# Cosformer attention and a mixture of adapters on one core: the written-out order of some 700 steps exchanged for another

## The chip, the cores and the metric

The kernel runs on 1 core of one Trainium2 chip. The metric is the device time of one execution in microseconds; what is given for a kernel is the median of several. The engines are called PE (TensorE: matmuls and transposes), DVE (VectorE), ACT (ScalarE), POOL (GpSimd) and SP (SyncE, which here issues every DMA). PEld is PE's loading of weights.

## The reference, cut to what matters

```python
B, H, S, D = 8, 8, 576, 64                     # q, k, v: [B, H, S, D], float32
theta = pi / 2 * arange(S) / S                 # c, s: its cosine and sine, one per position
phi = lambda x: concat([relu(x) * c, relu(x) * s], -1)
q_p, k_p = phi(q), phi(k)
kv  = einsum('bhsf,bhsd->bhfd', k_p, v)
z   = sum(k_p, axis=2)
attn = einsum('bhsf,bhfd->bhsd', q_p, kv) / (einsum('bhsf,bhf->bhs', q_p, z)[..., None] + 1e-6)

x = attn.transpose(0, 2, 1, 3).reshape(4608, 512)
logits = x @ w_gate                            # 8 experts
# the two largest logits of a row give the experts; w is their softmax
out = x + sum_over_the_two(w * (x @ A[e]) @ B[e])   # A[e]: 512 x 16, B[e]: 16 x 512
```

## The kernel before, in words

All eight heads of a batch lie side by side, and the 576 positions of a head are split as 64 partitions times 9 columns j, two heads' halves making 128 partitions. The batches come in load units: 0, 1, 2 and 3 alone, then 4 with 5 and 6 with 7 for q and k; v comes by single batches, but from batch 4 on its scaling treats two at once.

The work is cut into steps. `ops` holds each with its engines, its dependencies, the buffers that it takes and gives back, and a function that emits its instructions. The names, which the prediction uses:

| step | what it does | engine |
|---|---|---|
| `LKb`, `LQb`, `LVb`, `ldw` | loads of a unit of k, q, v; of the weights (L388, L356 to L361) | SP |
| `cKb.c`, `cQb.c` | a third of k or q cast to bf16, k with relu (L440, L442; L302 to L306) | DVE, ACT, for q also POOL |
| `phiKb.j`, `phiQb.j` | times tan: the sine half of a column (L310, L313) | POOL, DVE or ACT |
| `vsb.j` | a column of v times cos, as bf16 (L310, L313) | POOL, DVE or ACT |
| `kvb.c`, `keb` | 24 matmuls of batch b into two PSUM banks (L500); their copy to SBUF | PE; ACT or DVE |
| `tqi`, `eqi` | 8 transposes of phi(q) of tile i (L604); relu-copy of two tiles to SBUF (L621, L623) | PE; ACT or DVE |
| `ndi`, `rdi`, `nxi` | numerator and denominator of tile i (L647, L654, L662, L668); reciprocal; product, for two tiles (L692) | PE; DVE; DVE |
| `txi`, `exi` | 4 transposes of x (L713); copy of two tiles | PE; ACT or DVE |
| `zai` | x times A and w_gate (L738) | PE |
| `mxi`, `nt`, `ge`, `d`, `sg`, `w`, `zg` | largest logits (L749), their sum, mask, difference, sigmoid, weight, scaled z (L783), for three tiles; the last groups have two and one | DVE; `sg` ACT; `nt`, `w` DVE or POOL |
| `tz`, `ez` | transposes of the scaled z (L799); copy | PE; ACT or DVE |
| `dxi`, `eoi`, `sti` | x + z B in PSUM (L837); copy to the output buffer, two tiles wide or one; store (L855) | PE; ACT or DVE; SP |
| `fill=n` | n matmuls without use (L864) | PE |

There are 36 tiles of 128 rows: tiles 0 to 8 of batches 0 and 1, 9 to 17 of 2 and 3, 18 to 26 of 4 and 5, 27 to 35 of 6 and 7. Tiles 27 to 35 need `ke6` and `ke7`, that is the last loads V6 and V7 (`vs6.j` scales both at once).

The order is one text, `ORDER` (L68), read by `replay` (L127). In it `name=E@p` puts a step on engine E (V: DVE, S: ACT, G: POOL) and its result into place p of its buffers; a step without `=E` has one possible engine. Each engine gets its steps in the order of the text and runs them in that order; a step waits by semaphores for what it reads, and for the buffer that it overwrites. SP too works in order: a store whose tile is not ready holds all that stands behind it. Buffers that matter here: q has 4 places of a batch, k 4, v 3; PSUM has 8 banks; the output has 6 places, three of which lie in the first k tile and are free once batches 4 and 5 are cast. A place of the output is free again when its store has landed.

## Time and profile before

| | us |
|---|---|
| median of 3 runs | 119.18 (119.02 to 119.19) |
| the profiled execution | 118.97 |
| its span, first to last instruction | 117.2 |
| busy in the span: PE / PEld / DVE / ACT / POOL | 97.0 / 72.4 / 86.0 / 86.1 / 62.2 |
| granted TensorE clock, mean | 0.985 |

It moved 38.57 MB by DMA, 28.85 MB of it read from HBM. A store is 768 KB, but for two smaller ones at the end. To read the lines: a group of instructions gives line, engine, operation, what is written and read, shapes and count, then busy time in us and the mean ns of one, then the engine's idle time before them and what ended it. A line of the chain or of a timeline gives start, duration and what ran. "issue" is time in which an engine waited for nothing that the profile shows.

### The profile page before, as it was taken

Reading aid. Unit: us, or ns where it says so; the run is one execution under the profiler, and the core shown is the slowest. Engines: PE = TensorE matmul, PEld = TensorE weight load, DVE = VectorE, ACT = ScalarE, POOL = GpSimd, SP = SyncE. Lnnn points to the kernel's source line nnn. Section 1 sums busy time; section 2 is a strip of 40 time slices with the busy share of each in tenths; the row PEclk is TensorE's granted clock in tenths of the full one; section 3 lists DMA queues with packets and bytes.
Section 4 is the critical chain, followed back from the end, with each engine's and each line's share of the span. In section 5 each row is a group of like instructions: output and inputs, shape, how many; then the busy total and the mean of one; then the engine's idle time right before and its main releaser. Section 6 shows DMA issues by size and latency. Waiting matters only on the chain.

```text
span 117.2 us, 4510 instructions
## 1 busy us (share of the span) xinstructions
PE 97.0 (83%) x1930; PEld 72.4 (62%) x1939; DVE 86.0 (73%) x206; ACT 86.1 (73%) x132; POOL 62.2 (53%) x118
## 2 busy tenths in 40 slices
PE   5999687599885689698888969998879999999830
PEld 1344473479765586555767946787568797976300
DVE  1107878377958989799997886998499899987700
ACT  7328678479687797989838898777856666989750
POOL 3083707178889799379739954947993000011200
PEclk9999999976999999999999999999999999999999
DMA  2999999999999999999999999999810570493894
GB/s 42 401 399 391 390 392 392 392 304 395 392 389 391 391 391 391 385 393 389 388 393 385 392 385 391 388 417 424 363 56 6 233 299 19 168 369 163 336 394 187
DMA packets 15827, 38.57 MB, mean 329 GB/s; under 512 B 1728, under 2 KB 1728, under 8 KB 15808
## 3 DMA queue, kind: packets, MB, share of 16 engines
q1 hardware_dynamic: 15808, 38.29, 87.1%
q8 instruction: 15, 0.25, 0.9%
q14 instruction: 4, 0.03, 0.1%
HBM read 28.85 MB, written 9.44 MB: 327 GB/s over the span
## 4 chain that ended last, share of the span: by engine, by line
PE 32%; DMA 27%; DVE 21%; issue 6%; POOL 6%; ACT 2%; SPq 2%; DVEq 0%; POOLq 0%
DMA v<-in_v_dram 27%; PE psum L837 8%; PE psum L604 7%; PE psum L738 5%; DVE qt L623 5%; PE psum L713 4%; DVE x L692 4%; PE psum L654 3%; POOL vb L313 2%; POOL qp L304 2%; SPq L388 2%; DVE xt L306 2%; DVE kp L313 1%; DVE rd L687 1%; POOL qp L313 1%
## 5 line engine op out<-in xcount | busy, mean ns | idle before, releaser
L604 PE MATMUL psum<-ident,qp 128*128 128x128 bf16 x288 | 21.4, 226 | 4.1 <-DVE qp L313 1.3
L692 DVE TENSOR_TENSOR x<-psum,rd 128x1024 bf16<-128x1024 f32 (+1 forms) x19 | 22.2, 1168 | 0.6
L604 PEld LDWEIGHTS <-qp 128*128 128x128 bf16 x288 | 18.0, 101 | 6.1 <-issue 2.3
L313 POOL TENSOR_SCALAR kp<-kp,tanw 128x256 bf16<-128x256 bf16 (+1 forms) x28 | 16.2, 590 | 5.7 <-ACT kp L440 3.1
L313 POOL TENSOR_SCALAR qp<-qp,tanw 128x256 bf16<-128x256 bf16 (+1 forms) x31 | 17.2, 569 | 3.7 <-ACT qp L302 3.4
L313 POOL TENSOR_SCALAR vb<-v,cosw 128x256 bf16<-128x256 f32 (+1 forms) x25 | 14.8, 604 | 7.7 <-DMA v<-in_v_dram 7.6
L440 ACT ACTIVATE kp<-k 128x768 bf16<-128x768 f32 (+1 forms) x12 | 12.4, 1055 | 5.8 <-DMA k<-in_k_dram 5.4
L623 DVE TENSOR_SCALAR qt<-psum 128x2048 bf16<-128x2048 bf16 x12 | 14.6, 1214 | 0.9 <-PE psum L604 0.8
L713 PE MATMUL psum<-ident,x 128*128 128x128 bf16 x144 | 12.1, 221 | 3.3 <-DVE x L692 3.2
L500 PE MATMUL psum<-vb,kp 64*128 64x65 bf16 x576 | 12.8, 190 | 2.2 <-issue 1.1
L304 POOL CAST qp<-q 128x768 bf16<-128x768 f32 (+1 forms) x9 | 9.8, 1107 | 9.0 <-DMA q<-in_q_dram 7.4
L864 PE MATMUL psum<-ident 128*128 128x512 bf16 (+1 forms) x53 | 13.3, 405 | 1.4 <-POOL ident masks.py:199 1.4
L837 PE MATMUL psum<-x,ident 128*64 128x512 bf16 (+1 forms) x47 | 13.4, 384 | 0.6 <-ACT zt L302 0.3
L738 PE MATMUL psum<-AW,xt 128*128 128x136 bf16 x144 | 13.0, 223 | 0.7 <-DVE m L749 0.5
L500 PEld LDWEIGHTS <-kp 64*128 64x128 bf16 x576 | 10.2, 94 | 4.4 <-issue 2.4
L713 PEld LDWEIGHTS <-x 128*128 128x128 bf16 x144 | 9.3, 114 | 4.6 <-DVE x L692 4.3
L621 ACT ACTIVATE qt<-psum 128x2048 bf16<-128x2048 bf16 (+1 forms) x7 | 11.3, 1628 | 0.4 <-PE psum L604 0.4
L654 PE MATMUL psum<-kv,qt 128*64 128x65 bf16 x384 | 9.8, 197 | 2.1 <-issue 1.2
L837 PE MATMUL psum<-Bb,zt 128*64 128x512 bf16 (+1 forms) x42 | 11.4, 379 | 0.1
L302 ACT COPY o<-psum 128x1024 f32<-128x1024 f32 (+1 forms) x11 | 8.7, 821 | 3.7 <-PE psum L837 3.5
L738 PEld LDWEIGHTS <-xt 128*128 128x128 bf16 x144 | 9.4, 98 | 3.2 <-issue 1.4
L302 ACT CAST qp<-q 128x768 bf16<-128x768 f32 (+1 forms) x8 | 7.9, 987 | 4.7 <-DMA q<-in_q_dram 4.7
(60 smaller groups left out, 163.6 us busy)
## 6 DMA issues: line engine op xcount, KB each, us to landing
v<-in_v_dram SPq DMA_DIRECT2D x8, 1152.0 KB, 16.0
q<-in_q_dram SPq DMA_DIRECT2D x4, 1152.0 KB, 15.0
k<-in_k_dram SPq DMA_DIRECT2D x4, 1152.0 KB, 10.1
k<-in_k_dram SPq DMA_DIRECT2D x2, 2304.0 KB, 20.0
q<-in_q_dram SPq DMA_DIRECT2D x2, 2304.0 KB, 19.9
out_dram<-k SPq DMA_DIRECT2D x6, 768.0 KB, 4.5
out_dram<-o SPq DMA_DIRECT2D x5, 768.0 KB, 4.9
out_dram<-o SPq DMA_DIRECT2D x1, 512.0 KB, 2.7
```

What stands on the lines that cost most here:

```text
L302: nc.scalar.copy(o_ap, i_ap)
L313: eng.tensor_scalar(out=o_ap, in0=i_ap, scalar1=by, scalar2=0.0, op0=ALU.mult, op1=ALU.add)
L440: nc.scalar.activation(o_ap, i_ap, AF.Relu)
L500: nc.tensor.matmul(out=psum[:, s + hp, h2 * W:(h2 + 1) * W], lhsT=kp[hp * 64:hp * 64 + 64, bi * H2 + h2, :], rhs=vb_t[hp * 64:hp * 64 + 64 ...
L604: nc.tensor.transpose(out=o_ap[:, h2, :, hi, :], in_=qv[:, bi * H2 + h2, :], identity=ident)
L623: nc.vector.tensor_scalar(out=o_ap, in0=i_ap, scalar1=0.0, scalar2=None, op0=ALU.max)
L654: nc.tensor.matmul(out=psum[hi * 64:hi * 64 + 64, s + g, x * W:(x + 1) * W], lhsT=qt[:, qi, h2, hp, hi, :], rhs=kv_t[KV[b]["kv"].slot][:, ...
L692: nc.vector.tensor_tensor(out=x_t[Y["x"].slot][:, 0:n].rearrange("p n (g i d) -> p (n g) i d", g=2, i=4), in0=f()[:, :, :, 0:D], in1=r().t ...
L713: nc.tensor.transpose(out=bank16(s, 1024)[:, i * 512 + c * 128:i * 512 + (c + 1) * 128], in_=xv[:, c, :], identity=ident)
L738: nc.tensor.matmul(out=psum[:, s, i * ZW:(i + 1) * ZW], lhsT=xt_t[Z["xt"].slot][:, zi, c, :], rhs=AW[:, c, :], start=(c == 0 and i == 0), ...
L837: nc.tensor.matmul(out=o, lhsT=w, rhs=r, start=not last, stop=bool(last), skip_group_check=True)
L864: nc.tensor.matmul(out=psum[:, s % 8, c:], lhsT=ident, rhs=warm[:, c:], start=s < 8, stop=True, skip_group_check=True)
```

## The change

The text of `ORDER` is replaced; no other line differs. All steps of before are in it once, and the groups, tiles and matmuls are the same. What differs:

- the order of the steps on each engine, and the places in buffers and PSUM;
- the engine of some: `phiQ` of single batches runs 11 times on POOL, 9 on ACT, 16 on DVE (before 19, 10, 7), `phiK` 18, 11, 7 (15, 13, 8), `vs` 18, 12, 6 (16, 11, 9); of double units `phiQ` 9, 4, 5 (12, 5, 1), `phiK` 11, 4, 3 (13, 1, 4), `vs` 12, 4, 2 (9, 6, 3). `ex` runs 9 times on ACT and 10 on DVE (7 and 12), `ez` 4 and 9 (8 and 5), `eo` 21 and 3 (20 and 4), `eq` 7 and 12 as before, but other ones; `awb` is on POOL (ACT);
- five `fill` with 70 matmuls in all, instead of four with 55;
- the stores: before, `st8 st11 st14 st5` stand between the last load, `LV7`, and `kv6.0`, and then `st17 st20 st23 st2 st26 st29 st32 st35 st34`; now `st8 st14 st11 st17 st5 st2` stand there, and then `st23 st20 st26 st29 st32 st34 st35`.

The diff, cut to the first lines, those of `LQ4` and `LQ6`, and all from `LV7` on:

```diff
@@ ORDER @@
-half@3 ident fill=41@0 LQ0@3 LK0@0 LV0@0 pos tab LK1@1 LV1@1 LQ1@2 sig tan LQ2@1 ldw@2
-cQ0.0=S@0 cQ0.1=G@1 cQ0.2=G@2 LK2@2 phiQ0.5=G phiQ0.7=G LV2@2 cK0.2=S@1 cK0.1=V@2 cK0.0=V@3
...
-tx6@4 vs2.6=G d5 tx7 phiK2.7=S kv2.0@2 phiK2.3=G LV5@2 ex6=V@0 cK3.1=S@4 phiK2.8=G kv2.1 LQ4@2
...
-nd11 phiQ3.2=S kv3.0@0 fill=2@7 rd10@0 vs3.3=G LQ6@0 nx10@3 vs3.7=S vs3.5=G phiQ3.8=S nt8=G
...
-vs4.3=S kv4.0@0 vs4.7=G ez8=S@0 eq16=V@0 kv4.1 ex12=S@0 nt11=G kv4.2 LV7@1 d11 nd14@2 ke4=V@0
-sg11 nd15 w11=V dx6@0 rd14@1 nx14@6 dx7 dx8@6 eo6=S@4 cQ4.2=G@4 eo8=V nd16@2 tx14@0 zg11 st8.0
-tx15 za12@1 cQ4.0=G@2 ex14=S@1 nd17 mx12@2 kv5.0@6 rd16@2 nx16@7 za13 cQ4.1=S@0 za14 phiQ4.0=G
-kv5.1 mx13 mx14 kv5.2 phiQ4.1=S nt14=V phiQ4.4=G ge14 tq18@4 d14 ke5=V@2 sg14 phiQ4.7=G tq19
-phiQ4.2=S w14=V tx16@0 phiQ4.5=G tx17 zg14 eq18=S@1 ex16=V@0 tz14@6 phiQ4.3=G tz11@1 tq20@2
-ez11=V@1 za15@0 phiQ4.8=G cK6.0=V@2 tq21 ez14=S@2 cK6.2=S@0 nd18@4 dx11@1 eq20=V@0 phiK6.2=G
-nd19 cK6.1=S@4 phiK6.1=G mx15@1 dx9@2 rd18@0 dx10 nx18@0 za16 phiK6.5=G eo9=S@2 za17 mx16
-phiQ4.6=G tq22@4 mx17 nt17=V eo11=S tq23 d17 dx12@6 cQ6.0=G@0 sg17 st11.0 eq22=V@1 phiK6.3=S
-dx13 dx14@1 eo12=S@3 ge17 nd20@2 phiK6.6=G w17=V nd21 zg17 eo14=S tq24@6 phiK6.4=G rd20@2
-nx20@1 phiQ6.0=S tq25 st14.0 phiK6.0=G tx18@0 tx19 eq24=S@0 st5.0 phiK6.8=G ex18=V@0 nd22@2
-nd23 phiK6.7=V tq26@0 rd22@1 nx22@4 vs6.0=S@0,1 vs6.1=G za18@6 tx20@7 tx21 vs6.6=S tq27 vs6.2=G
-vs6.4=V tx22@2 tz17@3 vs6.3=S vs6.5=G tx23 ex20=V@1 za19 kv6.0@4 ez17=S@0 vs6.8=G ex22=V@0
-kv6.1 cQ6.2=S@2 za21@7 vs6.7=G eq26=V@1 dx15@2 cQ6.1=G@4 dx16 za20 mx18@1 eo15=S@5 za22 mx21@2
-za23 mx19 mx20 kv6.2 ge20 mx22 nt20=G phiQ6.2=V phiQ6.5=G nd24@0 ke6=S@1 d20 mx23 nd25 nt23=V
-sg20 kv7.0@4 d23 rd24@0 sg23 w20=G phiQ6.4=S nx24@2 phiQ6.7=G kv7.1 phiQ6.1=G kv7.2 ge23 w23=V
-phiQ6.8=G tq28@0 zg20 ke7=S@3 tq29 zg23 phiQ6.6=G tz20@6 nd26@2 eq28=V@0 ez20=S@1 nd27
-phiQ6.3=S dx17@7 rd26@0 dx18@0 nx26@5 eo17=S dx19 dx20@7 st17.0 eo18=S@4 tz23@6 nd28@2 eo20=V
-nd29 ez23=S@1 st20.0 tx24@0 rd28@0 tq30@6 nx28@3 tq31 tx25 tx26@1 ex24=S@0 eq30=V@0 tq32@2 tx27
-tq33 ex26=S@1 nd30@4 eq32=V@1 nd31 dx21@0 rd30@0 dx22 nx30@6 za24@2 eo21=S@2 za25 tx28@3 tx29
-za26 mx24@1 nd32@4 mx25 ex28=S@0 mx26 nt26=V nd33 ge26 d26 dx23@0 rd32@2 sg26 nx32@7 tq35@1
-w26=G eo23=S tq34@3 eq35=S@0 tx30@0 st23.0 tx31 zg26 za27@4 tx32@5 st2.0 ex30=V@1 za28 eq34=S@1
-za29 tz26@6 mx27@0 nd35@0 mx28 mx29 ez26=S@0 tx33 ge29 nt29=G rd35@0 za30@7 d29 dx24@2 nx35@0
-sg29 ex32=S@0 w29=G dx25 zg29 nd34@0 mx30@2 za31 eo24=S@5 rd34@0 za32 nx34@1 tz29@4 dx26@6
-ez29=S@1 mx31 za33@5 mx32 tx34@2 nt32=V eo26=S tx35@4 d32 dx27@0 mx33@1 ge32 sg32 st26.0
-ex34=V@1 dx28 ex35=S@0 w32=G za34 zg32 eo27=S@1 dx29@4 mx34 tz32@3 za35@6 nt34=G ez32=V@0
-eo29=S mx35@0 dx30@0 d34 nt35=G ge34 sg34 dx31 st29.0 d35 ge35 w34=G sg35 dx32@2 zg34 eo30=S@3
-w35=G zg35 eo32=V tz35@7 tz34@4 ez35=S@0 ez34=V@2 st32.0 dx35@7 dx33@0 eo35=S@0 dx34 st35.0
-eo33=S@2 st34.0
+half@3 ident fill=50@0 LQ0@3 LK0@0 LV0@0 pos tab LK1@1 LV1@1 LQ1@1 sig tan LQ2@0 ldw@2
+cQ0.0=V@0 cQ0.1=G@5 vone LK2@2 cQ0.2=G@3 phiQ0.1=G LV2@2 cK0.2=S@2 cK0.0=V@0 phiQ0.3=V
...
+phiK2.3=V tx4@2 tx6@3 phiK2.2=G eq8=V@1 sg2 LV5@2 tx5 tx7 phiK2.5=G cK3.2=S@1 kv2.0@4 LQ4@0
...
+vs3.2=G ez5=V@0 za8 cQ3.2=G@3 eq12=V@0 dx3@0 dx4 vs3.1=S vs3.4=G LQ6@2 dx5@6 mx6@0 eo3=S@2
...
+mx12@1 vs4.8=V nt11=G tx15 kv4.1 phiK4.8=V vs4.6=G ex14=V@1 eo8=S kv4.2 LV7@1 d11 mx13
+cQ4.0=S@4 cQ4.1=G@0 nd16@2 ge11 ke4=V@2 st8.0 nd17 za14 rd16@0 kv5.0@0 nx16@2 sg11 phiQ4.0=S
+w11=G phiQ4.2=G cQ4.2=S@2 kv5.1 phiQ4.4=V kv5.2 phiQ4.1=V mx14 tx16@2 phiQ4.5=V nt14=G tq18@4
+zg11 ke5=S@0 phiQ4.8=G tx17 tq19 ge14 d14 ex16=S@0 phiQ4.3=V za15@6 eq18=V@0 sg14 za16 w14=G
+za17 cK6.1=S@2 tz11@3 mx15@0 tq20@4 mx16 mx17 ez11=V@2 tq21 ge17 nd18@0 cK6.2=V@0 eq20=S@1
+phiK6.3=G zg14 nd19 phiK6.8=G nt17=V d17 tz14@7 rd18@2 sg17 tq22@4 phiK6.5=G ez14=S@0 nx18@1
+tq23 cK6.0=S@4 phiQ4.6=G dx11@7 w17=V dx9@2 eq22=V@0 dx10 phiK6.0=G tx18@0 eo9=S@3 tx19
+phiK6.4=V dx12@4 phiK6.7=G ex18=V@0 dx13 eo11=S cQ6.0=G@4 zg17 nd20@0 eo12=S@4 nd21 tz17@6
+rd20@0 za18@7 nx20@0 ez17=S@1 tq24@4 phiQ6.2=G phiK6.2=S dx14@6 cQ6.1=G@0 phiQ4.7=S nd22@0
+eo14=V nd23 mx18@0 tx20@6 st14.0 rd22@0 phiQ6.0=G tx21 phiQ6.3=S nx22@4 za19 st11.0 tq25
+phiQ6.1=G ex20=S@1 mx19 dx15@2 vs6.0=S@0,1 vs6.8=V vs6.4=G dx16 tq26@0 eq24=V@1 eo15=S@5 tq27
+vs6.5=G dx17@6 eq26=V@0 vs6.7=G nd24@2 eo17=S nd25 vs6.6=G phiK6.1=S za20 st17.0 rd24@0 tx22@6
+mx20 tq28@0 vs6.2=G vs6.1=S nx24@3 st5.0 tq29 nt20=G vs6.3=S tx23 st2.0 cQ6.2=G@2 d20 kv6.0@2
+ge20 sg20 ex22=V@0 phiQ6.4=S kv7.0@4 w20=V za21@6 phiK6.6=G eq28=S@1 zg20 za22 za23 mx21@1
+kv7.1 mx22 mx23 ge23 kv7.2 nt23=G d23 kv6.1 ke7=V@3 sg23 kv6.2 w23=G tz20@7 phiQ6.6=G zg23
+ke6=S@1 tq30@0 tz23@6 phiQ6.5=G ez20=S@2 nd26@2 ez23=V@0 nd27 phiQ6.8=V phiQ6.7=G dx18@6 rd26@0
+nx26@6 dx19 tq31 eo18=S@5 eq30=V@0 nd28@2 nd29 dx21@6 rd28@2 nx28@5 tx24@0 dx22 tx25 eo21=S@2
+tx26@1 tx27 ex24=V@0 nd30@2 nd31 dx20@0 rd30@1 nx30@2 tq32@6 eo20=S tq33 ex26=S@1 dx23@0
+eq32=V@1 za24@3 tx28@2 za25 eo23=S tx29 za26 mx24@2 ex28=S@0 nd32@4 st23.0 mx25 mx26 ge26 nd33
+nt26=V st20.0 d26 tq34@1 rd32@2 sg26 nx32@7 za27@0 w26=G eq34=S@0 tx30@2 za28 tx31 za29 mx27@1
+tx32@5 ex30=S@0 mx28 tx33 mx29 zg26 nd34@6 nt29=G ge29 ex32=S@1 tz26@4 rd34@0 tq35@1 d29 nx34@0
+za30@3 za31 sg29 ez26=V@0 za32 eq35=S@0 w29=G tx34@5 mx30@2 dx24@6 zg29 dx25 ex34=S@0 mx31 mx32
+tz29@4 nt32=V nd35@0 ge32 eo24=S@2 d32 ez29=V@1 dx26@5 rd35@0 za33@2 nx35@1 sg32 dx27@6 eo26=S
+w32=G dx28 zg32 st26.0 za34 eo27=S@1 mx33@0 tz32@4 mx34 dx29@3 ez32=V@2 nt34=G tx35@5 d34
+dx30@0 eo29=V ex35=S@0 dx31 ge34 sg34 st29.0 za35@4 eo30=S@4 w34=G dx32@6 mx35@1 zg34 nt35=V
+tz34@7 eo32=S ge35 ez34=V@2 d35 dx33@2 st32.0 sg35 dx34 w35=G zg35 eo33=S@2 tz35@0 ez35=V@0
+dx35@6 st34.0 eo35=S@0 st35.0
```

## Prediction

> **What bounds the kernel now.** I read the page first (its DMA digits: 40 slices of 2.93 us, 9 is full), then busy time by window, the chain of waits, and the SyncE timeline.

> ```profile
> DMA  2999999999999999999999999999810570493894
> ```
> ```profile
> 60.60:79.65 19.05, 16.87 (x404) 14.21 (x405) 15.91 (x35) 15.59 (x18) 13.78 (x17) 1.00 1.05 394
> 79.65:113.40 33.75, 30.22 (x631) 22.86 (x634) 26.59 (x71) 25.45 (x40) 10.68 (x21) 1.00 0.57 229
> ```
> ```profile
> 63.08 16.57 DMA v<-in_v_dram
> ...
> 112.33 1.01 ACT o L302
> ```
> ```profile
> 57.15 8.67 SPq L388 DMA_DIRECT2D v<-in_v_dram  x2
> 65.94 2.90 SPq L855 DMA_DIRECT2D out_dram<-k  x1
> ```

> The digits are 9 from the second slice to the 28th, up to 82 us: more than two thirds of the span run at the pace of the DMA engines. In the chain, the last load, V7, is issued at 63.08 and lands at 63.08 + 16.57 = 79.65. After it 33.7 us of computing remain, up to the last copy out of PSUM, 112.33 + 1.01 = 113.34; a store and the closing make it 117.2. The profiled execution took 118.97 us, 1.8 over its span and 0.2 under the median of 119.18. The windows list PE, PEld, DVE, ACT, POOL, the granted clock (1.00), DMA share and GB/s: in the tail PE is busy for 30.2 us of 33.75, DVE 26.6, ACT 25.5, POOL 10.7. No engine is full; they hand each tile round, every engine in a fixed order, and DVE has the longest list beside PE. So the time is V7's landing, plus this tail, plus the last store.

> **The loads do not move.** Both orders issue the same twenty loads (and the weights) in the same sequence, and all thirteen stores stand behind LV7 on SyncE. "Six stores instead of four" therefore means six stores ahead of kv6, none ahead of V7's bytes. V7 was issued 16.6 us before it landed: a load that a new buffer holds back must use up that lead first. LQ4 now waits for the casts of Q1 and Q2, and LV7 still for the scalings of V4 and V5, which in my walk end at about 59.5, as early as SyncE reaches LV7 in the row above. V7 lands at 79.7 in both.

> **Ahead of V7: does the work still fit?** The first cast of Q4 gives the start of the last stretch:

> ```profile
> 60.65 2.87 POOL L304 CAST qp<-q 128x1536 bf16<-128x1536 f32 x2 [2.69 <-DMA q<-in_q_dram]
> ```

> From here I summed each engine's steps up to its first step on V6, by the means of each kind. ACT has 15.5 us (13.6 before), POOL 12.2 (13.7), DVE the same as before within 0.1, and the window row shows that as 15.9 of 19.05. All fit. The 15 more filler matmuls lie ahead of V3's landing, where PE waits for loads; at 0.2 to 0.25 us each they would be 3 to 4 us on PE without that cover. The new order does more ahead of V6: za18, za19, tx20, tx21, ex20, tz17, ez17, cQ6.1 and three phiQ6; it leaves eq24, tq26, phiK6.1 and phiK6.6 for later.

> **The tail, walked by hand.** Durations, from the tail's groups by shape on DVE, ACT and POOL, the group of eq on ACT, and the chain for PE (x8 is one tq, two za, two tx; x2 one dx):

> ```profile
> L692 DVE TENSOR_TENSOR x<-psum,rd 128x1024 bf16<-128x1024 f32 x5 | 6.1, 1225 | 0.2
> L623 DVE TENSOR_SCALAR qt<-psum 128x2048 bf16<-128x2048 bf16 x4 | 4.9, 1218 | 0.2 <-PE psum L604 0.2
> L783 DVE TENSOR_TENSOR zg<-psum,w 128x384 bf16<-128x384 f32 x5 | 2.7, 549 | 0.1
> L749 DVE MAX8 m<-psum 128x8 f32<-128x8 f32 x18 | 2.4, 165 | 2.0 <-PE psum L738 1.8
> L306 DVE COPY xt<-psum 128x1024 bf16<-128x1024 bf16 x3 | 2.0, 684 | 0.2 <-PE psum L738 0.2
> ```
> ```profile
> L302 ACT COPY k<-psum 128x1024 f32<-128x1024 f32 x4 | 4.0, 1012 | 0.7 <-PE psum L837 0.6
> ...
> L302 ACT COPY o<-psum 128x512 f32<-128x512 f32 x3 | 1.8, 588 | 0.9 <-PE psum L837 0.7 <-PE psum L668 0.2
> ```
> ```profile
> L621 ACT ACTIVATE qt<-psum 128x2048 bf16<-128x2048 bf16 x5 | 9.3, 1867 | 0.4 <-PE psum L604 0.4
> ```
> ```profile
> L313 POOL TENSOR_SCALAR vb<-v,cosw 128x512 bf16<-128x512 f32 x5 | 3.7, 753 | 2.2 <-DMA v<-in_v_dram 2.2
> L313 POOL TENSOR_SCALAR qp<-qp,tanw 128x512 bf16<-128x512 bf16 x5 | 3.5, 720 | 0.0
> L304 POOL CAST qp<-q 128x1536 bf16<-128x1536 f32 x1 | 1.5, 1459 | 0.0
> ```
> ```profile
> 96.93 0.59 PE psum L837 x2
> 97.53 0.47 PE psum L738 x8
> 98.00 0.45 PE psum L713 x8
> ```

> Smaller steps, of 0.2 to 0.35 us, go in at their own means. For comparison the DVE timeline of before; the rows are nx24, nx26, nx32, then zg34 with zg35, and eo32:

> ```profile
> 86.44 1.23 DVE L692 TENSOR_TENSOR x<-psum,rd 128x1024 bf16<-128x1024 f32 x1
> ...
> 90.73 1.23 DVE L692 TENSOR_TENSOR x<-psum,rd 128x1024 bf16<-128x1024 f32 x1
> ...
> 99.75 1.22 DVE L692 TENSOR_TENSOR x<-psum,rd 128x1024 bf16<-128x1024 f32 x1
> ...
> 109.45 0.73 DVE L783 TENSOR_TENSOR zg<-psum,w 128x256 bf16<-128x256 f32 x2
> 110.10 0.68 DVE L306 COPY k<-psum 128x512 f32<-128x512 f32 x1
> ```

> After, from V7 on (times are ends):
> - DVE: vs6.8 80.5, eq24 81.6, eq26 82.7. PE waits for eq24, then nd24 and nd25 to 82.4; rd24 82.9, nx24 84.2. Before, nd24 stood behind kv6, and nx24 ended at 87.67: 3.5 us ahead here.
> - POOL: five scalings of V to 83.4, nt20 83.6, cQ6.2 85.0, phiK6.6 85.7. DVE: ex22 85.05. PE in a row: kv6.0, kv7.0, za21 to za23, kv7.1, kv7.2 (which needs phiK6.6), kv6.1, kv6.2, to 87.7. Tile 27 needs ke6 (88.4), and nd26 the banks of kv6 and kv7: here most of the 3.5 us is given back.
> - eq28 runs on ACT from 85.1 to 87.0 beside this; before, it was DVE's, directly ahead of nx26. nd26 and nd27 89.5, nx26 91.2 (before 91.96), eq30 92.3, nx28 93.8.
> - ex24 is DVE's now (0.68); nx30 96.4, eq32 97.5. Before, eq32 came ahead of nx30; now nd32 and nd33 wait for eq32, and nx32 ends at 100.4 (before 100.97): 0.6 ahead.
> - nx34 102.6; ACT: eo24 104.9, eo26 105.6; nx35 105.7, ex35 107.6, mx35 108.1, zg34 108.5, zg35 110.0 (before 109.45 + 0.73 = 110.18): 0.2 ahead.
> - The end. Before, eo32 (0.68) sat on DVE between zg35 and ez34, and dx33, dx34 and a wide eo33 came behind it: 110.18 to 113.34, 3.15 us. Now zg34, ez34, dx33 and dx34 lie in the wait for tile 35's sigmoid and product, eo32 is ACT's, and zg35 is followed by tz35 and ez35 (0.5, an estimate: an eighth of ex's columns), dx35 (0.35) and a narrow eo35 (0.59): 1.45 us, so 111.45. That gains 1.7 us.

> The last store leaves 0.2 + 1.7 = 1.9 us earlier.

> **What the walk leaves out** is PE standing at "issue", waiting for nothing that the profile shows:

> ```profile
> PEld L500 <- issue: 2.4, 5, 0.9
> PEld L604 <- issue: 2.3, 4, 1.0
> PEld L654 <- issue: 2.1, 3, 1.3
> ```

> (total us, times, longest.) L500 are the kv: 2.4 us over eight batches is 0.3 each. kv6 and kv7, with nothing behind them to hide a delay up to nx26, cost 0.6, and I add 0.1 for the rest of the way. Bounds: 0, if PE is waiting then anyway, and 2.4, all of L500's row. I take 0.7. [...]

> Forecast: 118.97 - 1.9 + 0.7 = **117.8 us**, its own range 117.0 to 118.6.

> **The rivals.**

> *A new wait for a store eats the gain.* eo33 now writes the buffer that eo26 filled last, so it waits until st26 has landed. Landing times of the stores in the tail, min, median, max:

> ```profile
> DMA to landing us min/median/max: 2.7/3.3/5.6
> ```

> eo26 ends at 105.6. With 3.3 the buffer is free at 109.0, and eo33, due at 109.85, doesn't notice. With 5.6 eo33 starts at 111.3 and the end is 1 us later; with a little more of "issue" that is 119.0, no change.

> *DVE reaches V7 late: slower.* The new order gives DVE 47 steps from SBUF to SBUF instead of 39, and beside POOL such a step takes longer:

> ```profile
> L313 DVE TENSOR_SCALAR kp<-kp,tanw 128x512 bf16<-128x512 bf16 x4 | 2.2, 570 | 0.0
> ...
> L313 DVE TENSOR_SCALAR qp<-qp,tanw 128x512 bf16<-128x512 bf16 x1 | 0.3, 343 | 0.0
> ```

> The same shape takes 343 ns in one place and 570 where POOL works on kp at the time. Nine such steps stand on DVE between V5 and V7; at 0.23 more each they are 2.1 us. With one PE stall of 1.3 ahead of an nx, and 1.0 of small waits, that is 4.4, against the 2.3 us that the walk leaves DVE before V7 (mx19 ends at 77.35): 2.1 late. Then eq24, nd24, za20 and mx20 are late; POOL, in order, holds nt20 and behind it cQ6.2 and phiK6.6; kv7.2, ke7 and tile 27 follow one for one: 119.9. It turns the gain into a loss from 1.4 us on, that is when nt20 ends after 85. For it: nothing in that chain can pass. Against it: the sums fit with 3 us to spare.
> [...]

> *The change isn't what it says*: did two stores pass ahead of V7, it would land later by two of 786 KB at the 394 GB/s of the window row, 4.0 us: 121.8. SyncE's order nearly excludes it.

> **How the numbers follow.** Forecast 0.62, new wait 0.13, DVE late 0.23, stores ahead 0.02. A measurement of this kernel tells about 0.2% (0.24 us) from no change. Faster is the forecast and half of the new wait (0.68); same is the other half and the edge of the third (0.08); slower the rest (0.24). The range runs from 116.6, the walk with no stall and 0.5 less of small waits than I put in, to 119.9, the time of DVE late.

> **What would show it.** V7 landing at 79.7; nx24 ending near 84.2, nt20 by 83.6; ke6 and ke7 done by 88.4; nx26 near 91; at the end one narrow copy of tile 35 that ends 1.5 us after the last zg. Should eo33 start over 0.3 us after dx34's end, the new wait is there. The prediction would be wrong with V7 landing late, with DVE still at its list ahead of V6 at 81, or with a PE stall over 1 us between 83 and 90, which moves all behind it.

## The result and the profile after

The changed kernel takes **118.00 us** (median of 4, 117.91 to 118.11); the kernel before, on the same chip, 119.12 (119.02 to 119.19). The ratio is 0.9907 (0.989 to 0.9924): 1.1 us faster, where 117.8 was forecast. The profiled execution took 118.06 us, 0.91 less than that of before, and its span is 116.3 (117.2). Each ratio here compares the fast executions alone; of the kernels below only the one with 24 idle matmuls fewer had slow ones, three of twelve.

Of after, the DMA digits of the page, two windows, and the chain of waits:

```profile
DMA  2999999999999999999999999999996001923994
```
```profile
60.60:79.65 19.05, 16.70 (x422) 13.52 (x414) 16.16 (x39) 16.65 (x21) 12.64 (x18) 1.00 1.05 396
79.65:112.50 32.85, 30.27 (x643) 22.84 (x640) 26.14 (x71) 24.23 (x36) 9.91 (x20) 1.00 0.59 236
```
```profile
63.30 16.49 DMA v<-in_v_dram
...
111.42 0.40 PE psum L837
111.83 0.02 issue
111.85 0.59 ACT o L302
```

V7 lands at 63.30 + 16.49 = 79.79, 0.14 behind before's. The DMA digits stay at 9 up to the thirtieth slice (28 before), since six stores now follow V7's bytes and not four. The tail ends at 111.85 + 0.59 = 112.44 with the copy of tile 35, 0.90 ahead of before's last copy. PE has the same work in the tail (30.27 against 30.22 us); the tail is shorter, and PE stands idle less.

The DVE timeline of after, the rows of nx24, nx26, nx28, nx32, then mx35, zg34, zg35 and the last ez:

```profile
82.84 1.22 DVE L692 TENSOR_TENSOR x<-psum,rd 128x1024 bf16<-128x1024 f32 x1
...
89.63 1.23 DVE L692 TENSOR_TENSOR x<-psum,rd 128x1024 bf16<-128x1024 f32 x1
...
92.84 1.23 DVE L692 TENSOR_TENSOR x<-psum,rd 128x1024 bf16<-128x1024 f32 x1
...
99.19 1.23 DVE L692 TENSOR_TENSOR x<-psum,rd 128x1024 bf16<-128x1024 f32 x1
...
108.60 0.17 DVE L749 MAX8 m<-psum 128x8 f32<-128x8 f32 x1 [0.56 <-PE psum L738]
108.69 0.41 DVE L783 TENSOR_TENSOR zg<-psum,w 128x256 bf16<-128x256 f32 x1
...
110.53 0.29 DVE L783 TENSOR_TENSOR zg<-psum,w 128x128 bf16<-128x128 f32 x1 [0.62 <-POOL w L780]
111.14 0.23 DVE L306 COPY zt<-psum 128x128 bf16<-128x128 bf16 x1 [0.32 <-PE psum L799]
```

Against before: nx24 starts 3.6 us earlier, nx26 1.1, nx32 0.56. zg35 is done at 110.82, 0.64 later than before's zg34 with zg35, and what stands behind it takes 1.62 us where before it took 3.16.

Between nx26 and nx28 PE's weight loads stand still inside nd28:

```profile
90.43 0.11 PEld L654 LDWEIGHTS <-qt 128*64 128x64 bf16 x1
90.91 0.20 PEld L654 LDWEIGHTS <-qt 128*64 128x64 bf16 x8 [0.37 <-issue]
91.84 0.20 PEld L654 LDWEIGHTS <-qt 128*64 128x64 bf16 x7 [0.73 <-issue]
```

The brackets give the idle time ahead of the row and what ended it. "issue": for 0.73 us PE waits for nothing that the profile shows, in the middle of sixteen loads that are all alike. (The 0.37 ahead of it is another matter: it stays where the 0.73 goes.)

### The profile page after: what moved, and what is told of

It reads as the page before. It is cut to its first block, busy times and chain, and to the rows that moved or that the text cites. A ratio compares the mean times of both kernels' runs of the same rounds, so it can differ in the third digit from the quotient of the medians.

```text
span 116.3 us, 4552 instructions
## 1 busy us (share of the span) xinstructions
PE 98.2 (84%) x1954; PEld 73.5 (63%) x1954; DVE 86.1 (74%) x211; ACT 84.1 (72%) x126; POOL 62.6 (54%) x119
## 4 chain that ended last, share of the span: by engine, by line
PE 36%; DMA 29%; DVE 14%; ACT 8%; SPq 4%; issue 4%; POOL 1%; POOLq 0%; DVEq 0%; ACTq 0%
DMA q<-in_q_dram 14%; DMA v<-in_v_dram 14%; PE psum L604 8%; DVE x L692 6%; PE psum L837 6%; PE psum L738 5%; PE psum L713 5%; SPq L388 4%; PE psum L654 4%; PE psum L500 4%; DVE qt L623 3%; ACT o L302 2%; PE psum L647 2%; ACT qt L621 2%; PE psum L799 1%
## 5 line engine op out<-in xcount | busy, mean ns | idle before, releaser
L604 PE MATMUL psum<-ident,qp 128*128 128x128 bf16 x288 | 21.5, 226 | 1.9 <-DVE qp L313 1.8
L692 DVE TENSOR_TENSOR x<-psum,rd 128x1024 bf16<-128x1024 f32 (+1 forms) x19 | 22.2, 1168 | 1.1 <-PE psum L864 0.6
L313 POOL TENSOR_SCALAR kp<-kp,tanw 128x256 bf16<-128x256 bf16 (+1 forms) x29 | 16.7, 587 | 10.0 <-ACT kp L440 10.0
L604 PEld LDWEIGHTS <-qp 128*128 128x128 bf16 x288 | 18.2, 102 | 3.1 <-DVE qp L313 1.9
L313 POOL TENSOR_SCALAR vb<-v,cosw 128x256 bf16<-128x256 f32 (+1 forms) x30 | 17.6, 604 | 3.1 <-DMA v<-in_v_dram 3.1
L864 PE MATMUL psum<-ident 128*128 128x512 bf16 (+1 forms) x70 | 16.4, 388 | 1.4 <-POOL ident masks.py:199 1.4
L623 DVE TENSOR_SCALAR qt<-psum 128x2048 bf16<-128x2048 bf16 x12 | 14.5, 1219 | 1.3 <-PE psum L604 1.2
L713 PE MATMUL psum<-ident,x 128*128 128x128 bf16 x144 | 12.5, 221 | 3.0 <-DVE x L692 2.8
L304 POOL CAST qp<-q 128x768 bf16<-128x768 f32 (+1 forms) x10 | 11.2, 1128 | 6.3 <-DMA q<-in_q_dram 6.3
L302 ACT COPY o<-psum 128x1024 f32<-128x1024 f32 (+1 forms) x12 | 9.9, 840 | 6.4 <-PE psum L837 6.2
L837 PE MATMUL psum<-x,ident 128*64 128x512 bf16 (+1 forms) x48 | 13.9, 385 | 0.6 <-DVE x L692 0.6
L837 PE MATMUL psum<-Bb,zt 128*64 128x512 bf16 (+1 forms) x48 | 13.8, 379 | 0.3 <-DVE zt L306 0.2
L713 PEld LDWEIGHTS <-x 128*128 128x128 bf16 x144 | 9.8, 114 | 6.1 <-DVE x L692 2.5
L738 PE MATMUL psum<-AW,xt 128*128 128x136 bf16 x144 | 12.7, 223 | 0.9 <-ACT xt L302 0.4
L621 ACT ACTIVATE qt<-psum 128x2048 bf16<-128x2048 bf16 (+1 forms) x7 | 11.4, 1628 | 2.2 <-PE psum L604 2.1
L313 POOL TENSOR_SCALAR qp<-qp,tanw 128x256 bf16<-128x256 bf16 (+1 forms) x20 | 11.5, 583 | 2.7 <-DVE qp L306 2.5
L500 PE MATMUL psum<-vb,kp 64*128 64x65 bf16 x576 | 11.7, 190 | 1.4 <-issue 0.6
L864 PEld LDWEIGHTS <-ident 128*128 128x128 bf16 x70 | 7.0, 104 | 9.1 <-issue 2.4
L780 POOL TENSOR_TENSOR w<-ge,ex 128x24 f32<-128x24 f32 (+2 forms) x10 | 2.3, 231 | 18.8 <-ACT ex L776 18.7
L500 PEld LDWEIGHTS <-kp 64*128 64x128 bf16 x576 | 9.9, 94 | 3.2 <-issue 1.5
L654 PE MATMUL psum<-kv,qt 128*64 128x65 bf16 x384 | 9.8, 197 | 2.1 <-issue 1.6
```

The costliest lines, as they stand in the source:

```text
L313: eng.tensor_scalar(out=o_ap, in0=i_ap, scalar1=by, scalar2=0.0, op0=ALU.mult, op1=ALU.add)
L500: nc.tensor.matmul(out=psum[:, s + hp, h2 * W:(h2 + 1) * W], lhsT=kp[hp * 64:hp * 64 + 64, bi * H2 + h2, :], rhs=vb_t[hp * 64:hp * 64 + 64 ...
L604: nc.tensor.transpose(out=o_ap[:, h2, :, hi, :], in_=qv[:, bi * H2 + h2, :], identity=ident)
L621: nc.scalar.activation(o_ap, i_ap, AF.Relu)
L623: nc.vector.tensor_scalar(out=o_ap, in0=i_ap, scalar1=0.0, scalar2=None, op0=ALU.max)
L654: nc.tensor.matmul(out=psum[hi * 64:hi * 64 + 64, s + g, x * W:(x + 1) * W], lhsT=qt[:, qi, h2, hp, hi, :], rhs=kv_t[KV[b]["kv"].slot][:, ...
```

## The experiments

Each kernel was compared with the kernel before on the same chip, in five rounds. Which parts bring the 1.1 us? Two kernels cross the orders at vs6.0, the first step on V6; two cross them at the last 17 steps. In these four the lines of the code have numbers lower by 2.

**The front of before, the tail of after.**

```diff
-(after's text up to vs6.0)
+(before's text up to vs6.0)
+tz17 za18 ez17 phiQ6.2 cQ6.1 mx18 tx20 tx21 phiQ6.3 za19 phiQ6.1 ex20 mx19 dx15
 vs6.0=S ...
 (the steps still missing, in after's order)
```

> Before's order and engines up to vs6.0 (the first step on V6), after's for all that is left. Theory A, what is done ahead of V6 is paid for by waiting for loads, and the order from V7 on decides: V7 lands at 79.7 and the time is 118.0 to 118.4, near after. Theory B, the gain comes from what the new order has done by the time V7 lands: 118.8 to 119.2, near before.

With this edit the 14 steps that only after has ahead of vs6.0 stand there too, behind all of before's front.

Measured: 119.00 us, ratio 0.9992 (0.997 to 1.0014): no gain, as theory B had it. Its DVE timeline at nx24, and PE's row of nd24:

```profile
83.86 0.26 DVE L685 RECIPROCAL rd<-psum 128x16 f32<-128x16 f32 x1 [0.93 <-PE psum L666]
84.13 0.17 DVE L747 MAX8 m<-psum 128x8 f32<-128x8 f32 x1
84.22 1.21 DVE L690 TENSOR_TENSOR x<-psum,rd 128x1024 bf16<-128x1024 f32 x1
```
```profile
82.95 0.44 PE L652 MATMUL psum<-kv,qt 128*64 128x65 bf16 x16 [0.85 <-ACT k L300]
```

nx24 is 1.4 us later than in after, nx32 ends 1.24 later, eo35 1.24 later: after's tail, shifted as a whole. nd24 waits 0.85 us for one of ACT's copies out of PSUM. ACT also has before's eq24 ahead of V6 here, which after gives to DVE behind vs6.8. So it isn't enough that ex20, za18, za19 and their like stand ahead of vs6.0; which of the front's differences makes it late, the run doesn't say.

**The front of after, the tail of before.**

```diff
 (after's text up to vs6.0)
+phiK6.1 phiK6.6 eq24 st5.0 tq26
-(after's order of the rest)
+(before's order of the rest)
```

> After's order up to vs6.0, before's for the rest, the mirror of the run with before's front. Theory A: 118.8 to 119.2, near before. Theory B: 117.9 to 118.3, near after.

Measured: 119.49, ratio 1.0038 (1.0023 to 1.0053), above the ranges of both theories. nx24 starts at 86.66, as late as before's, because nd24 stands behind kv6; eo33 ends at 113.81. So after's front with before's tail brings nothing either: the gain belongs to the pair. That the front clears the way and a tail with nd24 ahead of kv6 uses it fits both runs, but isn't shown, since nd24 was not moved by itself and both kernels have more ahead of vs6.0 than either order.

**The last 17 steps alone, and all but them.**

```diff
 ... zg34
-(one kernel's last 17 steps)
+(the other's)
```

> Before up to zg34, after's order and engines for the last 17 steps: tz34, ez34, dx33, dx34 ahead of zg35, eo32 on ACT, a narrow eo35 last. Theory C, the prediction's term: the end order alone gains 1.7 us, 117.4. Theory D: before's zg34 and zg35 follow each other closely, so the wait in which after hides tile 33 and 34 isn't there; then eo33 (1.0) and eo35 (0.6) line up on ACT, the last copy ends near 113.0 instead of 113.34, and 0.3 to 0.4 us are gained, 118.75.

Measured: 119.67, ratio 1.0045 (1.0032 to 1.0058). ACT's timeline:

```profile
109.82 1.50 ACT L300 COPY k<-psum 128x1024 f32<-128x1024 f32 x2
112.43 1.50 ACT L300 COPY o<-psum 128x1024 f32<-128x1024 f32 x2 [1.11 <-PE psum L835]
```

Both theories missed it: a loss of 0.55 where they had gains. eo33 starts at 112.43, no earlier than before's 112.33, and eo35 now stands behind it on ACT.

> After up to zg34, then before's last 17 steps: zg34 and zg35 in a row, eo32 on DVE ahead of ez34, dx35 ahead of dx33, eo33 last. Theory C, the end order alone is worth 1.7 us: 119.6. Theory D: zg35 comes earlier than in after (110.05 instead of 110.82), eo33 ends near 112.9 instead of eo35 at 112.44, and 0.4 to 0.5 us are lost, 118.45.

Measured: 118.80, ratio 0.9981 (0.9969 to 0.9992), between the theories' 118.45 and 119.6: with before's end, 0.8 of the 1.1 us are lost. (Here nt35, d35, ge35 and sg35 stand ahead of zg34, as in before.) So the end is worth 0.8 behind after's body and minus 0.55 behind before's; the body alone is worth 0.3. The parts don't add up, each needs the other.

**Four stores behind V7 again.**

```diff
-... nx24@3 st5.0 tq29 ... tx23 st2.0 cQ6.2=G@2 ... st20.0 d26
+... nx24@3 tq29 ... tx23 cQ6.2=G@2 ... st20.0 st5.0 st2.0 d26
```

(Besides, eo21, eo24, eo30, eo33 and eo35 write to other places of the output.)

> The changed order, but st5.0 and st2.0 lie behind st20.0 on the SP queue again, so that four stores and not six stand among and right behind the last loads. Theory S (the two extra stores keep the DMA engines full past 89 us, and that is why the weight loads of nd28 stand still for 0.73 us at 91.8 us): the stall in nd28 goes, rd28 and rd30 no longer wait, nx32 ends before 100.42 us, and the time is 117.5 to 118.0. Rival (the stall doesn't depend on the queue's load there): it stays at about 0.7 us in nd28, and the time is 118.0 as it is for the changed order, within 0.1.

Measured: 118.10, ratio 0.9921 (0.9908 to 0.9934), no gain. Yet the stall is gone. The weight loads at nd28:

```profile
90.42 0.11 PEld L654 LDWEIGHTS <-qt 128*64 128x64 bf16 x1
90.95 0.33 PEld L654 LDWEIGHTS <-qt 128*64 128x64 bf16 x15 [0.42 <-issue]
```

The 0.42 stays, the 0.73 is away, and everything from nx28 to the last copy is 0.6 to 0.8 us earlier (nx32 ends at 99.65, eo35 at 111.67 instead of 112.44). What is saved is given back in the DMA queue: busy time by window (last two columns: DMA share, GB/s) of this kernel, then of after:

```profile
103.50:106.00 2.50, 2.50 (x39) 1.70 (x39) 1.93 (x7) 1.99 (x4) 0.23 (x1) 1.00 0.86 341
```
```profile
103.50:106.00 2.50, 2.50 (x36) 1.50 (x35) 2.29 (x10) 2.31 (x5) 0.24 (x1) 1.00 0.02 7
```

The old stores, issued at 99 us, fill the time up to 107; the new stores queue behind them, and from issue to landing the last five take 3.4 to 4.5 us instead of 2.7 to 3.4. The last store lands at 115.10, in after at 115.17. The theory on the stall held, and the last section shows the packet of the instruction queue behind which load 1634 stalls in after; that it would show in the time did not.

**Two stores ahead of V7.**

```diff
-... kv4.2 LV7@1 d11
+... kv4.2 st5.0 st2.0 LV7@1 d11
```

(st5.0 and st2.0 are taken out where they stood.)

> The changed order, but st5.0 and st2.0 are issued on SP ahead of the load of V7. Theory L (the end is V7's landing plus a tail with no room ahead of nx24): the two stores of 786 KB together push V7's landing from 79.8 us back by about 2 us for one and 4 us for both (at the near 394 GB/s of the full DMA engines), so V7 lands at 81.8 to 83.8 us and the time is 119.5 to 122. Rival (the DMA engines serve the store beside the load, or there is room behind V7): V7 lands less than 1 us later or the tail takes it up, and the time is 118.0 to 118.8.

Measured: 122.29, ratio 1.0275 (1.0253 to 1.0298), 4.3 us over the changed kernel and 0.3 over the expected range. In its chain, and in a window behind V7 (the third value from the end is the granted clock):

```profile
66.73 16.80 DMA v<-in_v_dram
83.53 0.03 issue
83.56 0.49 DVE vb L313
```
```profile
85.00:87.00 2.00, 1.77 (x46) 1.75 (x47) 1.56 (x3) 2.00 (x5) 2.00 (x4) 0.50 0.83 344
```

V7 lands at 83.53 and not 79.79, so 3.7 later, and eo35 ends 4.1 later. The end is V7's landing plus the tail; nothing takes up any of it. The tail even grew, though the stall in nd28 is gone: PE stood idle for 4.14 us, until DVE had got V7 and done eq24, and behind that the granted clock was 0.50 up to 88 us (1.00 in after). nx26 ends 4.9 later than in after.

**eq28 back on DVE.**

```diff
-eq28=S@1
+eq28=V@1
```

> The changed order with one engine changed back: eq28 is done by DVE (1.22 us in the kernel before) and not by ACT. Theory B (DVE's list between V7 and nx26 has little room, so this copy's engine is a part of the gain): nx26 ends about 0.7 us later than 90.85, nx32 some 0.3 to 0.7 later than 100.42, and the time is 118.3, between 118.0 and 118.7. Rival (all 1.2 us of DVE is on the path): 119.1 or more. Rival (DVE has room there): 118.0, no change.

Measured: 118.02, ratio 0.9907 (0.9894 to 0.992), no change. nx26 ends 0.43 later (91.28), but nd28's stall is 0.19 here instead of 0.73, and nx28 ends at 93.95, earlier than after's 94.07. The run doesn't say what eq28's engine would cost without the stall; with it, nothing.

**Another order of the last steps.**

```diff
-eo29=V ex35=S@0 ... zg34 nt35=V tz34@7 eo32=S ge35 ez34=V@2 d35 dx33@2 st32.0 sg35 ... eo35=S@0
+eo29=S ex35=V@0 ... mx35 nt35 d35 zg34 ge35 sg35 tz34 eo32 w35 ez34 dx33 ... eo35=V@0
```

> The changed order, with ex35 and eo29 and eo35 on the engines that are free (ex35 on DVE, eo29 on ACT, eo35 on DVE), and the last steps ordered so that d35 lies ahead of ez34 and ge35, sg35 are not behind it. Theory E (after nx35 the changed order loses 1.0 us against the walk, through mx35's wait for ex35 and zg35's wait for the weight scaling of d35): zg35 starts some 0.5 us earlier than 110.54, and the time is 117.4 to 117.7. Rival (the end hangs on tiles 33 and 34, whose copies eo33 and eo34 stand in line on ACT and DVE): eo33 ends no sooner than 111.8 and the time stays at 118.0, within 0.2.

Measured: 118.43, ratio 0.9934 (0.9921 to 0.9946): 0.4 slower than after, and above both ranges. zg35 starts at 110.15, 0.38 earlier (0.5 expected). But ez34 gets behind d35, zg34 and ge35, dx33 starts at 109.62 instead of 109.22, and eo33 ends at 112.20 instead of 111.81. Tiles 33 and 34 and tile 35 compete for DVE's last microsecond; what one gains the other loses.

**The old stores behind st20.**

```diff
-... nx24@3 st5.0 ... tx23 st2.0 ... eo21=S@2 ... eo20=S ... eo23=S ... st23.0 ... st20.0 ...
+... nx24@3 ... tx23 ... eo21=S@1 ... eo20=S st20.0 st5.0 st2.0 ... eo23=S st23.0 ...
```

> The changed order, but on the SP queue st20.0 comes ahead of st23.0 and the two old stores st5.0 and st2.0 stand right behind st20.0, so that they are issued at about 95.5 us (when eo20 is done) and not at 82.5 us; eo21 takes another place. Theory D (with four stores behind V7 the stall in nd28 goes and the last copy ends 0.77 us earlier, but the two old stores, issued at 99 us, push the last stores back by as much; the DMA engines lie idle from about 88 to 97 us, where there is room): the stall stays away, the old stores land before 103.5 us, the last copy ends at about 111.7 us, the last store lands at about 114.4 us, and the time is 117.2 to 117.5. Rival (the engines being full from 95.5 to 104 us, the stall only moves to a later weight load, or eo24 waits for the place of st2.0): 118.0, within 0.2.

Measured: 117.73, ratio 0.9882 (0.9866 to 0.9897). The stall stays away, and nx35 ends 0.70 earlier than in after; but the last copy ends at 112.14, only 0.30 earlier. ACT's timeline at eo27:

```profile
106.30 1.01 ACT L302 COPY o<-psum 128x1024 f32<-128x1024 f32 x1 [1.12 <-DMA out_dram<-o]
```

eo27 waits for the place that st23.0 leaves when it lands.

**The same, with another place for eo27.**

```diff
-eo27=S@1
+eo27=S@5
```

> The kernel with st20.0 first and st5.0 and st2.0 behind it, but eo27 writes to the place that st20.0 has left (it landed at 99.56 us there) and not to that of st23.0 (landed at 106.22 us, 0.7 us later than eo27 could have started). Theory D, as before: with that wait gone the last copy ends at about 111.7 us and not at 112.14 us, the last store lands at about 114.4 us, and the time is 117.2 to 117.5. Rival (something else in the end takes up the 0.4 us, dx33 and eo33 or the queue of the stores): 117.7, within 0.15.

Measured: **117.25**, ratio 0.984 (0.9828 to 0.9853), against 0.989 to 0.9924 for the changed kernel: the fastest version here, 0.75 us under it. The same row, and this kernel's DMA digits:

```profile
105.60 1.02 ACT L302 COPY k<-psum 128x1024 f32<-128x1024 f32 x1 [0.51 <-PE psum L837]
```
```profile
DMA  2999999999999999999999999999950006993994
```

eo27 now waits for PE alone. The last copy ends at 111.64 and the last store lands at 114.39, as expected. The two old stores now lie from 96 to 104 us, where after's digits were 1, 9 and 2 (here 6, 9 and 9): behind the place of the stall, and not in the way of the last stores.

**24 idle matmuls more.**

```diff
-fill=3@12 ... fill=8@10 ... fill=2@8
+fill=11@12 ... fill=16@10 ... fill=10@8
```

> The changed order with 24 idle matmuls more (8 each at three fills at 29, 35 and 41 us, in gaps of 1.5 us in which TensorE waits for DVE), so that every later step stands 24 weight loads further on in TensorE's instruction stream. Theory F (the long stalls come at fixed places of the stream, the 994th, 1122nd, 1506th or 1634th weight load, 128 apart, and only while the DMA engines are full): in the new count the stalls stand at the same numbers, that is 24 weight loads earlier in the work (the stall of nd28 moves from the 1634th load, which is then nd28's no more, to the step 24 loads ahead of it, in rd26 or nd26 or nd27), of 0.4 to 1.2 us; the time is 117.7 to 118.4. Rival (the stalls belong to the steps, by what they wait for): they stay with the same steps, at the 1018th, 1146th and 1658th load, and the time is 118.0.

Measured: 123.96, ratio 1.0411 (1.0365 to 1.0456). The numbers of the stalls came out as theory F had them: the loads 994, 1122 and 1634, with 738 (0.47) as a fourth. (Loads are counted from 0, together with the two or three drain and semaphore instructions that PEld's record has ahead of them; without these the numbers are 991, 1119, 1631 and 735.) Number 1634 is now in another place of the work, among the small loads of L668 at the end of nd27:

```profile
92.26 0.11 PEld L668 LDWEIGHTS <-ident 128*64 128x64 bf16 x1
95.26 0.14 PEld L668 LDWEIGHTS <-ident 128*64 128x64 bf16 x3 [2.88 <-issue]
```

The time was missed by 5.5 us, for two reasons. The stall is 2.88 us, not 0.4 to 1.2. And the gaps that I filled were not free; DVE's timeline of this kernel, then of after:

```profile
30.54 0.26 DVE L687 RECIPROCAL rd<-psum 128x16 f32<-128x16 f32 x1 [2.33 <-PE psum L864]
```
```profile
29.68 0.26 DVE L687 RECIPROCAL rd<-psum 128x16 f32<-128x16 f32 x1 [1.59 <-PE psum L864]
```

rd2 waits for L864, the idle matmuls, which write other columns of the bank that it reads. Each eight more push the next product back by 0.85 us (nx2 0.85, nx6 1.73, nx8 2.61). That front is 2.8 us late at vs6.8, though V7 lands at 79.88.

**24 idle matmuls fewer at the start.**

```diff
-fill=50@0
+fill=26@0
```

> The changed order with 26 idle matmuls at the start and not 50, so that every later step stands 24 weight loads earlier in TensorE's instruction stream; nothing waits for these matmuls but the first real ones. Theory F: the stalls keep their numbers in the stream (994, 1122, 1634), that is, they stand 24 loads later in the work; the 1634th comes at 92.0 us or later, when the DMA engines have been empty since 91.5 us, and is gone or under 0.3 us; nx32 ends at about 99.7 us, the time is 117.3 to 117.8. Rival 1 (the stalls belong to the steps): they stand at the 970th, 1098th and 1610th load, nd28 still loses 0.7 us, 118.0. Rival 2 (the stream's stall comes all the same, longer, as in the run with 24 more): 118.0 to 119.5. The shorter start may lower the granted clock of the first 20 us, where the loads set the pace: nothing is expected from that.

Measured: 119.05, ratio 0.9986 (0.9964 to 1.0007); single executions spread from 118.55 to 122.01, so the places tell more here than the time. The stalls stand again at fixed numbers: 738 (2.52 us), 994 (1.68), 1122 (1.03), 1506 (0.71), and none at 1634. The 1506th load, in kv:

```profile
87.91 0.27 PEld L500 LDWEIGHTS <-kp 64*128 64x128 bf16 x13
88.90 0.51 PEld L500 LDWEIGHTS <-kp 64*128 64x128 bf16 x29 [0.71 <-issue]
```

Theory F held for the places and rival 1 fell. The time came out as rival 2 had it (118.0 to 119.5, by longer stalls): vs6.8 is 0.7 us late, and the front's lead is what this order lives on. The stalls ahead of V7 are longer, but they are not the only difference: the granted clock was 0.50 from 14 to 20 us, behind 3.0 us without a matmul, where after had 1.00. What each cost isn't shown.

## Why the prediction was right, step by step

- *The loads do not move.* Right: V7 landed at 79.79, forecast 79.7. The kernel with two stores ahead of it shows what hung on it: 3.7 us of landing became 4.3 of time.
- *The work ahead of V7 fits.* Right: DVE waits 0.78 us for V7 ahead of vs6.8. It had less to spare than the 2.3 us of the walk (mx19 ended at 79.11, not 77.35). The rival that DVE comes late didn't occur; the kernel with before's front, in which DVE reaches its step on V6 at 80.49 and then waits for PE, is the nearest to it, 1.0 us slower than after.
- *The walk of the tail.* Right within 0.35 us on DVE up to nx35: nx24 84.07 (84.2 forecast), nx26 90.85 (91.2), nx28 94.07 (93.8), nx30 96.67 (96.4), nx32 100.42 (100.4), nx35 105.76 (105.7). ke6 and ke7 were done by 88.09 (88.4). But that agreement holds two errors. The run with four stores shows the same steps without the stall: nx32 at 99.65. So the walk was 0.75 too slow there, and the stall, which the walk left out, made it up: that was luck.
- *"Most of the 3.5 us is given back" and eq28 on ACT.* The first held (nx26 is 1.1 ahead). The second has no price as things are: on DVE it made no difference.
- *0.7 for "issue".* The size was right, 0.73 in one stall that the four-store run shows to cost 0.77 at the last copy. The place was wrong: not kv6 and kv7, but nd28, and the reason isn't kv but the count of the instruction. That the size agrees is luck too: it was worked out for kv6 and kv7.
- *The end.* The one term that was mis-sized: "That gains 1.7 us" behind zg35 came out at 3.16 - 1.62 = 1.54, but zg35 itself ended at 110.82 and not 110.0. From the end of nx35 to the last copy it is 6.68 us, where the walk had 5.75; without the stall it is 6.67. DVE's rows name the waits: 0.56 ahead of mx35, for PE, and 0.62 ahead of zg35, for the weights of tile 35. The other order of the last steps took 0.38 off zg35 and lost 0.39 at eo33. What would take both waits away I didn't find.
- *The rival of a new wait for st26.* Not there: st26 landed at 109.16, eo33 started at 110.79 behind PE. The mechanism is real, though: eo27 ran into it when the stores moved.

So 1.9 less 0.7, that is 1.2, was forecast for the profiled execution, and 0.9 came: the 0.7 was as large as stated, in another place; the walk had 0.75 too much in its middle and 0.9 too little at its end. The mechanism (V7's landing, a shorter tail, a better end, some stalling) held; that the sum came within 0.3 owes much to errors that cancel.

The prediction's lower bound for the stalls, 0, gives 118.97 - 1.9 = 117.1, and can now be weighed as well: without the stall in nd28 and without the jam of stores, it is 117.25, though that kernel also has two stores in another order.

## What to carry to other kernels

Reordering gains where two pieces fit, so cross the pieces before crediting one: here the front, the tail and the end each gave nothing or a loss beside the other order's rest. When stores must be put off, look at the DMA digits for a stretch that is empty anyway, and check who waits for the places that they leave. A stall in the middle of equal instructions, with no semaphore, can be a matter of the instruction's number (here 0.73 us at load 1634): count it in two kernels, and look at the packets of the instruction queue, before explaining it by the step.

## What the runs showed of the hardware

```profile
q8 instruction: 15, 0.25, 0.9%
```
```profile
q1 hardware_dynamic: 194, 1.01, 85.4%
```
```profile
q1 hardware_dynamic: 17, 0.09, 18.8%
q8 instruction: 1, 0.02, 5.5%
```

15 packets and 0.25 MB, 16,384 bytes each in the packed traces of before and after. For the 1954 matmuls and as many loads of after that is 261 instructions per packet if all are PE's, an estimate; the spacing of the stalls, 256, is near it.

The packed traces give each packet's start and duration too. A block here is the 128 loads from one such number to the next, with their matmuls, and blocks and packets are paired in order (in before and after the first packet ends ahead of load 226, the 14th ahead of load 1890). In after, PE begins the block at load 1506 at 86.47. The packet of the next block starts 2.99 us later, with the DMA share at 0.84 meanwhile, and ends at 90.42; load 1634, the first of that block, goes at 91.84, 1.43 later. In the kernel with four stores the packet starts 0.73 us after load 1506 (DMA share 0.06), and there is no stall. Taken over the 14 traces: no block begins sooner than 1.23 us after its packet has ended (the least in before and after is 1.30), and at all 40 stalls of 0.19 us or more at these numbers it begins 1.23 to 1.53 us after (1.42 to 1.50 at the six of before and after). In before and after, with the DMA share below 0.1 meanwhile, the packet starts 0.38 to 1.40 us after the beginning of the block before (four times); with a share of 1 or more, 1.71 to 3.86 us after it (21 times); with shares from 0.39 to 0.88, 0.78 to 2.99 us (four times; one more packet starts after 0.04 us, too short for a share).

So PE stalled in these traces where it was through with a block sooner than 1.2 to 1.5 us after the end of the next one's packet. From load 994 to load 1122 it always did: the time between them was 6.19 to 6.20 us in 12 of the 14 kernels and 6.47 in two, while the stall in it went from 0.44 to 1.32. In after that is 3.69 until the packet starts, 1.04 for the packet and 1.46 behind it. At loads 866, 1250 and 1378 PE was slower than the packets, and nothing over 0.12 was lost. At load 1506 before lost 0.94, though its DMA engines emptied on the way: the packet started 1.85 us behind load 1378 and ended at 86.36, the block began 1.43 us after that, 4.25 us behind load 1378, and PE's work up to there took only 3.31. In after the same packet ended 1.37 us ahead of load 1506, and nothing was lost.

Of the 196 crossings from one block to the next in these traces 156 lost less than 0.19 us; the other 40 cost PE 0.19 to 2.88 us each (in before and after six of 28, 0.43 to 1.27 us).

**Idle matmuls are waited for.** With 24 more narrow ones in the bank of the next reciprocal, nx8 came 2.61 us later than in after, 0.11 for each.
